# Moving a transform table's second half and its transposes to a later place in the opening of a fused FFT and channel-mix kernel

## The chip, the cores and the metric

The kernel runs on one core of a Trainium2 chip. The metric is device time in microseconds (us), the median of several executions. The kernel before takes 593.0 us.

## The reference

For x of 8 batches x 3072 positions x 256 channels: a real FFT along the positions, a complex matrix product with a soft threshold, the inverse FFT, then a channel mix in the manner of RWKV.

```python
X = np.fft.rfft(x, axis=1)
Yr = Xr @ w_r - Xi @ w_i + b_r            # and Yi = Xr @ w_i + Xi @ w_r + b_i
Yr = np.sign(Yr) * np.maximum(np.abs(Yr) - 0.01, 0.0)      # the same for Yi
x = np.fft.irfft(Y, n=3072, axis=1)
# channel mix: x_prev is x moved by one position
xk, xr = mu_k * x + (1 - mu_k) * x_prev, mu_r * x + (1 - mu_r) * x_prev
v = np.maximum(xk @ w_k, 0.0) ** 2 @ w_v
return v / (1.0 + np.exp(-(xr @ w_r)))
```

## The kernel before

The FFT of length 3072 is done as 96 x 32: a first stage with the 96-point table FT, a second with the table G (and G0 for the group of frequency zero), the product, an inverse second stage with the table GI (the transposes of G, scaled), and an inverse first stage. G is made in the kernel by two sines on ScalarE, one for each half; GI is made from it by 24 transposes on TensorE and three copies out of PSUM.

The program is written out by a small list scheduler in Python. Every piece of TensorE work is a `Unit` with what it needs, a due time and an assumed duration; the loop issues the unit with the earliest due time among those that are ready by the assumed clock. So assumed times do not change what is computed, but they set the order of instructions on every engine. Each unit takes one of four slots of PSUM and gives it back when its copy has run; `copy` gives that copy to ScalarE or VectorE, whichever is free first by the assumed clock. The parts that matter (cuts are marked `...`):

```python
    def make_g():
        nc.scalar.activation(G[:, :, :, 1, :], ang, AF.Sin, bias=0.0, scale=sc1)   # second sine
        nc.vector.tensor_scalar(out=G0[:, 0], in0=G[:, 0, 1], scalar1=-1.0, scalar2=None, op0=ALU.mult)
        nc.vector.tensor_copy(out=G0[:, 1], in_=G[:, 0, 0])
        nc.vector.memset(G0[:, 0:2, 0, 0:1], 0.0)
        nc.vector.tensor_copy(out=G0[:, 2:4], in_=G[:, 0])
    ...
    def table_gi(n):
        def issue(ps, h, end):
            for i in range(8):                                   # eight transposes of G
                nc.tensor.matmul(ps[:, 128 * i:128 * i + 128], G[:, 8 * n + i]..., ident, ...)
            def evac(k):
                nc.scalar.activation(GI[:, 8 * n:8 * n + 8, :], ps..., AF.Copy, bias=0.0, scale=float(1.0 / 32))
                ...
                if n == 0:                                       # two corrections of one row each
                    for r in (0, 64):
                        nc.vector.tensor_scalar(out=GI[r:r + 1, 0, :], in0=GI[r:r + 1, 0, :], scalar1=0.5, ...)
    def tables(k):
        nc.scalar.activation(G[:, :, :, 0, :], ang, AF.Sin, bias=0.0, scale=sc0)   # first sine
        at(run_on("act", k, 1.5) + 0.3, tables1)
    def tables1(k):
        make_g()
        e = run_on("act", k, 1.5)
        done["G"] = run_on("dve", e, 0.5)
    ...
    for q in range(4):
        done["x", 0, q] = 6.0 + 2.8 * q                          # assumed arrival of x, batch 0
    tab += [Unit(18.0 + n, 0.5, ["G"], table_gi(n)) for n in range(3)]
```

In batch 0 a piece of x goes through the first stage (L327 of the kernel before), its result is copied into the tile YT, 48 transposes in six units (L345) turn it, copies put them into the tiles A, then come the second stage (L370 and L387), a copy and a sign turn of XT (L397), the first product (L415), and z (L427) on VectorE. In the changed kernel the same lines have numbers lower by one.

## Time and profile before

| | kernel before |
|---|---|
| median, lowest, highest of 6 runs | 593.00, 592.49, 593.43 us |
| span of the profiled execution | 592.2 us |
| TensorE, VectorE, ScalarE busy | 566.3, 524.1, 420.2 us |
| TensorE without a matmul, 12.76 to 24 us | 1.53 us of 11.24 |
| VectorE starts on z of batch 0 | 25.40 us |

The span is the time from the first to the last instruction of one execution. "Busy" adds the instructions of one engine. The last two rows are about the opening, the only part that the change touches; the prediction below shows the lines that they come from. The profiled execution took 593.96 us by the clock outside, longer than each of the six timed runs.

### The profile page before, as it was taken

The numbers are of one execution on the slowest core, as the hardware profiler recorded it, in microseconds if no ns is written. First come the engines' busy times: TensorE is split into PE (matmuls) and PEld (weight loads), VectorE is DVE, ScalarE is ACT, GpSimd is POOL, SyncE is SP. The second block draws the span as 40 slices with busy tenths as digits, with TensorE's granted clock in tenths as the row PEclk, the third lists the DMA queues.
The fourth block names the chain that finished last, engine by engine and source line by source line (L and its number), as shares of the span: only waits on it lengthen the run. The fifth ranks groups of instructions, "written<-read, shape, count | busy, mean of one in ns | idle before, by whom it ended". The sixth has DMA issues, their size and how long they took to land.

```text
span 592.2 us, 12299 instructions
## 1 busy us (share of the span) xinstructions
PE 566.3 (96%) x4822; PEld 429.7 (73%) x4889; DVE 524.1 (89%) x833; ACT 420.2 (71%) x457; POOL 26.3 (4%) x56
## 2 busy tenths in 40 slices
PE   3999899999999999999999999999999999999996
PEld 3888666777767777677777777677877787776665
DVE  7799989798998889898998989988999889979883
ACT  4686967677777687676777677777776867767652
POOL 7101000000000000000000000000000000000000
PEclk9999999999999999999999999999999999999999
DMA  8976879724589365963478655683337722362223
GB/s 132 139 145 159 189 178 240 179 71 93 132 208 217 102 142 137 253 182 69 113 169 250 149 121 129 160 238 112 99 93 236 179 55 72 100 169 70 64 56 97
DMA packets 69594, 84.38 MB, mean 142 GB/s; under 512 B 9121, under 2 KB 54560, under 8 KB 69536
## 3 DMA queue, kind: packets, MB, share of 16 engines
q1 hardware_dynamic: 62912, 68.98, 41.7%
q0 software_dynamic: 6432, 14.36, 16.5%
q8 instruction: 38, 0.62, 0.4%
q10 hardware_dynamic: 192, 0.26, 0.2%
q14 instruction: 20, 0.16, 0.1%
HBM read 50.73 MB, written 47.19 MB: 165 GB/s over the span
## 4 chain that ended last, share of the span: by engine, by line
PE 82%; DVE 6%; ACT 5%; issue 2%; DMA 2%; SPq 1%; POOL 1%; POOLq 0%; DVEq 0%; ACTq 0%
PE banks L671 27%; PE banks L627 23%; PE banks L415 13%; PE banks L654 5%; PE banks L454 3%; PE banks L387 3%; PE banks L272 3%; ACT rl L633 2%; PE banks L535 2%; DMA Adr<-A 1%; ACT rg L659 1%; PE banks L345 1%; SPq L297 1%; DVE k L639 1%; DMA out_dram<-o 1%
## 5 line engine op out<-in xcount | busy, mean ns | idle before, releaser
L633 ACT ACTIVATE rl<-banks 128x1024 bf16<-128x1024 f32 x192 | 193.6, 1028 | 94.0 <-PE banks L627 88.2
L627 PE MATMUL banks<-xk,wk 128*128 128x512 bf16 x701 | 188.7, 379 | 5.3 <-DVE xk L600 0.7
L671 PE MATMUL banks<-wv,k 128*128 128x256 bf16 x1536 | 183.0, 272 | 0.4 <-ACT rl L633 0.3
L671 PEld LDWEIGHTS <-k 128*128 128x128 bf16 x1536 | 149.3, 98 | 29.0 <-issue 1.4
L639 DVE TENSOR_TENSOR k<-rl 128x1024 bf16<-128x1024 bf16 x192 | 130.5, 685 | 13.9 <-ACT rl L633 13.9
L627 PEld LDWEIGHTS <-wk 128*128 128x128 bf16 x768 | 73.9, 98 | 60.7 <-issue 3.1
L415 PEld LDWEIGHTS <-XT 128*128 128x128 bf16 x768 | 74.5, 98 | 15.5 <-DVE XT L397 0.3
L415 PE MATMUL banks<-wi,XT 128*128 128x256 bf16 x384 | 73.3, 273 | 0.0
L415 PE MATMUL banks<-wr,XT 128*128 128x256 bf16 x384 | 73.3, 272 | 0.0
L600 DVE SCALAR_TENSOR_TENSOR xk<-diff,muk,YT 128x512 bf16<-128x512 bf16 x96 | 69.1, 745 | 0.2
L600 DVE SCALAR_TENSOR_TENSOR xr<-diff,mur,YT 128x512 bf16<-128x512 bf16 x96 | 68.8, 745 | 0.0
L682 DVE TENSOR_TENSOR o<-banks,rg 128x1024 f32<-128x1024 f32 (+1 forms) x49 | 58.6, 1197 | 3.7 <-PE banks L671 3.4
L219 ACT ACTIVATE YT<-banks 128x768 bf16<-128x768 f32 x56 | 42.7, 829 | 10.8 <-PE banks L535 7.9
L219 ACT ACTIVATE XT<-banks 128x1024 bf16<-128x1024 f32 (+2 forms) x45 | 42.8, 956 | 10.6 <-PE banks L387 10.6
L654 PE MATMUL banks<-wrm,xr 128*128 128x256 bf16 x384 | 49.8, 272 | 0.1
L659 ACT ACTIVATE rg<-banks 128x1024 bf16<-128x1024 f32 x48 | 49.1, 1023 | 0.0
L432 ACT ACTIVATE z<-banks 128x1024 bf16<-128x1024 f32 x32 | 32.7, 1022 | 19.9 <-PE banks L415 19.8
L654 PEld LDWEIGHTS <-xr 128*128 128x128 bf16 x384 | 37.2, 98 | 11.6 <-issue 0.2
L219 ACT ACTIVATE V<-banks 128x1024 bf16<-128x1024 f32 x35 | 35.9, 1025 | 13.5 <-PE banks L454 12.8
L219 ACT ACTIVATE A<-banks 96x1024 bf16<-96x1024 f32 (+1 forms) x39 | 39.3, 1021 | 7.3 <-PE banks L272 6.0
L594 DVE TENSOR_TENSOR diff<-YT 128x1024 bf16<-128x1024 bf16 x48 | 32.8, 683 | 3.7 <-ACT YT L219 3.7
L444 DVE TENSOR_TENSOR Y<-z,Y 128x1024 bf16<-128x1024 bf16 x48 | 33.2, 693 | 1.7
(90 smaller groups left out, 443.1 us busy)
## 6 DMA issues: line engine op xcount, KB each, us to landing
out_dram<-o SPq DMA_DIRECT2D x188, 128.0 KB, 2.2
xs<-in_x_dram POOLq DMA_DIRECT2D x32, 384.0 KB, 6.2
Vdr<-V SPq DMA_DIRECT2D x192, 64.0 KB, 1.8
V<-Vdr SPq DMA_DIRECT2D x32, 384.0 KB, 6.5
Adr<-A SPq DMA_DIRECT2D x24, 384.0 KB, 5.4
A<-Adr SPq DMA_DIRECT2D x48, 192.0 KB, 4.4
wk<-in_moe_w_k_dram POOLq DMA_DIRECT2D x1, 512.0 KB, 15.1
wv<-in_moe_w_v_dram POOLq DMA_DIRECT2D x1, 512.0 KB, 15.9
```

Of the source, the lines that this page charges most:

```text
L219: nc.scalar.activation(out, in_, AF.Copy, bias=0.0, scale=1.0)
L415: nc.tensor.matmul(o, lhs, w[:, c, :], start=(w is wr and c == 0), stop=(w is wi and c == NCD - 1))
L444: nc.vector.tensor_tensor(out=y, in0=z, in1=y, op=ALU.subtract)
L594: nc.vector.tensor_tensor(out=df, in0=y, in1=yp, op=ALU.subtract)
L600: nc.vector.scalar_tensor_tensor(out=m[:, c, :], in0=df[:, c, :], scalar=mu[:, c:c + 1], in1=yp[:, c, :], op0=ALU.mult, op1=ALU.add)
L627: nc.tensor.matmul(ps[:, 512 * f:512 * f + 512], wk[:, c, 128 * ff:128 * ff + 128], xk[:, c, :], start=(c == 0), stop=(c == NCD - 1))
L633: nc.scalar.activation(rl, ps, AF.Relu, bias=0.0, scale=1.0)
L639: nc.vector.tensor_tensor(out=k2, in0=rl, in1=rl, op=ALU.mult)
L654: nc.tensor.matmul(ps[:, 256 * q:256 * q + 256], xr[:, c, 128 * q:128 * q + 128], wrm[:, c, :], start=(c == 0), stop=(c == NCD - 1))
L659: nc.scalar.activation(rg, ps, AF.Sigmoid, bias=0.0, scale=1.0)
L671: nc.tensor.matmul(ps[:, 256 * q:256 * q + 256], K2[t][:, ff, 128 * q:128 * q + 128], wv[:, ff, :], start=(ff == 0), stop=(ff == NCF - 1))
L682: nc.vector.tensor_tensor(out=o[:, lo:hi], in0=ps[:, lo:hi], in1=rg[:, lo:hi], op=ALU.mult)
```

## The change

The intent: to let the data's transposes start as soon as the data is there, instead of behind the table's. The second sine is issued as before, but the four G0 instructions of VectorE are put behind it in a step of their own; x of batch 0 is assumed to arrive every 2.55 instead of 2.8 us; and the table's transposes also wait, in the schedule, for the last copy of the first stage.

```diff
--- before.py
+++ after.py
@@ -155,8 +155,7 @@
     G = const.tile([128, NG, 2, 2, 32], FP16, name="G")
     G0 = const.tile([128, 4, 2, 32], FP16, name="G0")
 
-    def make_g():
-        nc.scalar.activation(G[:, :, :, 1, :], ang, AF.Sin, bias=0.0, scale=sc1)
+    def make_g0():
 
         nc.vector.tensor_scalar(out=G0[:, 0], in0=G[:, 0, 1], scalar1=-1.0, scalar2=None, op0=ALU.mult)
         nc.vector.tensor_copy(out=G0[:, 1], in_=G[:, 0, 0])
@@ -737,9 +736,12 @@
         at(run_on("act", k, 1.5) + 0.3, tables1)
 
     def tables1(k):
-        make_g()
-        e = run_on("act", k, 1.5)
-        done["G"] = run_on("dve", e, 0.5)
+        nc.scalar.activation(G[:, :, :, 1, :], ang, AF.Sin, bias=0.0, scale=sc1)
+        at(run_on("act", k, 1.5), tables2)
+
+    def tables2(k):
+        make_g0()
+        done["G"] = run_on("dve", k, 0.5)
 
     P = 71.5
     START = 50.0
@@ -777,7 +779,7 @@
                             [("k2", t, i) for i in range(4)] + [("rg", t)], v_unit(t, p), part=p))
 
     for q in range(4):
-        done["x", 0, q] = 6.0 + 2.8 * q
+        done["x", 0, q] = 6.0 + 2.55 * q
         load_x(1, q)
         done["x", 1, q] = 19.0 + 3.0 * q + (4.0 if q > 1 else 0.0)
         if q == 1:
@@ -787,7 +789,7 @@
     done["FT"], done["bias"] = 5.0, 21.0
     at(12.0, tables)
     tab = [Unit(18.0, 0.1, ["FT"], table_fi)]
-    tab += [Unit(18.0 + n, 0.5, ["G"], table_gi(n)) for n in range(3)]
+    tab += [Unit(18.0 + n, 0.5, ["G", ("x1", 0, 3, 1)], table_gi(n)) for n in range(3)]
     streams = [tok, val, fa, fb, fc, tab]
     at(START - 10.0, lambda k: mix_tokens(0, k))
```

## The prediction

> **What bounds the kernel now.** I read the page's head first, for which engine fills the span.
>
> ```profile
> span 592.2 us, 12299 instructions
> ...
> PE 566.3 (96%) x4822; PEld 429.7 (73%) x4889; DVE 524.1 (89%) x833; ACT 420.2 (71%) x457; POOL 26.3 (4%) x56
> ```
>
> TensorE is busy for 566.3 of 592.2 us, so all its idle time is 25.9 us. The change only touches how the tables G, G0 and GI are made, once, in the first 25 us. So next I cut the span into stretches (columns: stretch, its length, then busy time of PE, PEld, DVE, ACT, POOL, the granted clock, DMA share, GB/s).
>
> ```profile
> 12.76:24.00 11.24, 9.71 (x110) 9.20 (x110) 8.20 (x15) 9.56 (x10) 3.93 (x6) 1.00 1.11 95
> 24.00:45.00 21.00, 19.53 (x239) 17.09 (x237) 19.85 (x29) 15.34 (x18) 0.00 (x0) 1.00 0.83 163
> ...
> 145.00:520.00 375.00, 370.95 (x3078) 279.79 (x3124) 340.19 (x529) 276.22 (x299) 7.10 (x14) 1.00 0.58 149
> ```
>
> From 145 to 520 us TensorE is idle for only 4.05 us of 375. A microsecond won before 25 us therefore reaches the end, and nothing later can be won. The stretch that the change rewrites, 12.76 to 24 us, has 11.24 - 9.71 = 1.53 us of idle TensorE. Third, the chain that ended last, in that stretch (start, us, what):
>
> ```profile
> 12.66 0.98 ACT G L736
> 13.64 0.50 issue
> 14.14 1.57 ACT G L159
> 15.71 0.05 issue
> 15.76 1.89 PE banks L717 x16
> 17.64 3.34 PE banks L345 x32
> 20.98 0.22 PE banks L370 x2
> 21.20 0.93 PE banks L387 x14
> 22.12 0.60 PE banks L717 x8
> 22.72 0.89 PE banks L345 x16
> 23.62 1.76 PE banks L415 x16
> 25.38 0.02 issue
> 25.40 1.24 DVE z L427
> ```
>
> The reader is to see the order: both sines on ScalarE (L736, L159), then 16 of the 24 table transposes (L717), then the transposes of the data (L345), the second stage (L370, L387), and the first product (L415). TensorE stands still for 1.53 us until the second sine ends. The number to beat is 25.40, where VectorE starts on the first product's result; the next chain hangs on that.
>
> Fourth, the groups by form, first of 15.7 to 20.8 us, then of 20.8 to 27.5 us:
>
> ```profile
> L345 PE MATMUL banks<-ident,YT 128*128 128x128 f16 x32 | 3.5, 311 | 0.0
> L717 PE MATMUL banks<-ident,G 128*128 128x128 f16 x16 | 1.9, 312 | 1.5 <-ACT G L159 1.5
> ```
>
> ```profile
> L387 PE MATMUL banks<-G,A 128*128 128x128 f16 x22 | 1.7, 219 | 0.0
> ```
>
> The same 128x128 product takes 312 ns early and 219 ns later. Spacing matters more: 16 + 32 products fill 15.76 to 20.87 us, 5.11 / 48 = 0.107 us each, while the 8 that start at 22.12 have the next group's first start at 22.56 in the timeline: 0.44 / 8 = 0.055 us each. A unit of eight transposes so costs 0.85 us early and 0.44 us later.
>
> **What the Trainium skill says.** "TensorE: Matmul & The Clock Gate", part 1, the clock gate: matmuls of 128 columns come every 106.7 ns while the array is cold and every 55.6 ns once warm, and the array warms after some 3.4 us of sustained activity, in windows that run freely and do not start with the kernel. The trace agrees in the two spacings; the array warms at about 20.7 us, 4.9 us after the dense work began at 15.76, which fits one whole busy window plus a part of one. The granted clock in the table above reads 1.00 throughout and does not show it. The same page's table of specifications says that ScalarE and VectorE execute strictly in order. That is what lets a late table instruction hold up a data instruction; the trace shows each engine's instructions in the order of the program. "ScalarE: Activation LUTs", "Table sets: the hidden batching unit", says that cheap functions such as copy are in every set; so copies may stand between the two sines without a new table load. The trace agrees: sine, copy and sine alternate there with one load of 1.28 us at 0.74 us and the next at 42.74 us, for the sigmoid.
>
> **The change, part by part.** The order listing, with line numbers made equal, has the same instructions in the same number on every engine; GpSimd and the DMA queue have the same order, and TensorE, VectorE and ScalarE differ only up to the first product of batch 0. Nothing is removed or added.
>
> (1) ScalarE takes the copy of the third x piece before the first sine and the copy of the fourth between the sines. The first sine cannot move up: it waits for the angle that VectorE finishes at 12.63 us. The copy's matmuls end at about 11.75, so it runs 11.79 to 12.6 (0.8 us) and the sine starts at 12.66 as before. The second sine slips from 14.14 to 14.84 and ends at 16.4.
>
> (2) VectorE is relieved of one of three copies of 0.95 us. The fourth x piece ends on TensorE at 14.22; ScalarE copies one half 14.14 to 14.93, VectorE the other 14.26 to 15.21. Before, that last copy ran at 16.14 to 17.09, behind the G0 instructions.
>
> (3) So L345 starts at 15.27 in the place of L717 at 15.76: 0.49 us earlier. All 48 data transposes go first, six units of 0.85 us if cold: 15.27 to 20.39. Copies follow: VectorE's first 16.37 to 17.6, then the G0 group of 0.45 us, units 4 and 6 at 18.93 to 20.16 and 20.64 to 21.87; ScalarE's at 17.22 to 18.24, 18.14 to 19.16 and 19.78 to 20.80.
>
> (4) L370 runs at 20.39 to 20.61 (warm assumed), its copy on ScalarE 20.84 to 21.45; six L387 to 20.94, copy to 22.2. Then the first eight L717 wait for a PSUM slot, that of data unit 5, free at 20.80: 20.95 to 21.4. Sixteen of the 24 transposes are now warm: 16 x (0.107 - 0.055) = 0.83 us of TensorE time is saved, and 0.49 of an earlier start. That is 1.3 us, if TensorE stayed the bound.
>
> (5) It does not. Three GI copies on ScalarE, one every 0.92 us, come behind the XT copy at 22.2: the first ends at 23.14. The first product (L415) takes the slot which that copy frees, so it starts at 23.2, against 23.45 before. And VectorE now has in its order: two corrections of GI (0.44 us, waiting for that same copy), then the sign turn of XT (0.26), a copy of 1.23 and another turn of 0.28. From 23.18 these end at 23.6, 23.85, 25.05 and 25.25. L415 needs the turn only at its seventh matmul, at 23.86, so it is hardly delayed and ends at 25.1. VectorE is free for z at 25.25. Against 25.40 that is a gain of 0.15 us.
>
> From there the orders are the same, so I carry 0.15 us to the end, and add 0.1 for waits that I rounded up: 592.96 - 0.25 = 592.7 us.
>
> **The rivals.** *The full gain.* If ScalarE's table copies fit into its idle time, TensorE would stay the bound and 1.3 us would come through: 591.7. For it: ScalarE is idle 1.7 us of the 11.2 in this stretch, and TensorE's total work is less. Against it: the GI copies stand ahead of what the first product waits for, in both engines' order; in the kernel before two of the three were done by 18.8 us, while TensorE was busy with data. I give it one in six.
>
> *The wait turns into a loss.* If the array warms later, at 22 us instead of 20.7, L370, L387 and the first L717 run cold, about 0.5 us more on the chain of (4) and (5): 593.2. For it: the free-running window, and TensorE now has short gaps at 20.4 to 23.2, where before it was dense. Against: 15.27 to 20.39 alone holds a full window in most phases. One in four. The three runs of the kernel before, 592.49 to 593.43, spread by 0.94 us, as much as a window's phase could explain.
>
> *A transfer hides it.* The first wait for x in the chain is untouched, as the DMA order is. The loads of the next batch arrive before TensorE asks at 35.7 us, so a lead of some tenths should not hit them. If it did, the result would be 592.96 again.
>
> **Range and chances.** 0.15 to 0.25 us is under the spread of one kernel's runs. I take plus 0.8 and minus 0.9 around 592.7: 591.8 at the low end (nearly the full gain), 593.5 at the high end (late warming and a slow median). A change of 2% would be 11.9 us; all idle TensorE time before 45 us is under 12, and 6.3 of that is before any data. So faster by over 2%: 0.003; slower by over 2%: 0.003, only if the order broke something far later; within 2%: 0.994.
>
> **What would show it.** Step 1: second sine starts near 14.85. Step 3: first L345 near 15.3, with no L717 before it. Step 4: all 24 L717 at 219 ns rather than 314. Step 5: the GI corrections on VectorE waiting for ScalarE, and the first L415 at about 23.2, z at about 25.25. The busy sum of TensorE should fall by some 16 x 0.1 = 1.6 us at most, since the products overlap, without the span following. The prediction is wrong if z starts before 24.7 or after 25.8, if an instruction order differs after 26 us, or if a gain or loss at 28 us is not the same at 145 us.

## The result, and the profile after

| | before | after |
|---|---|---|
| median of 6 runs | 593.00 us | 592.71 us |
| lowest to highest | 592.49 to 593.43 | 592.30 to 593.16 |
| span of the profiled execution | 592.2 us | 591.0 us |
| data transposes in full pace of issue from | 17.43 us, behind 16 of the table's | 15.35 us, nothing ahead |
| first product starts | 23.45 us | 22.74 us |
| z starts | 25.40 us | 25.01 us |

The ratio is 0.9995, with a 95% interval of 0.9983 to 1.0008: the same time. All ratios here are the mean time of one kernel's fast runs over that of the other's of the same rounds, so not quite the ratio of the medians that I quote.

The same stretch of the chain that ended last, in the changed kernel (start, us, what):

```profile
14.34 0.97 DVE YT L220
15.31 0.05 issue
15.35 4.18 PE banks L344 x39
19.54 0.02 issue
19.56 0.69 ACT A L218
20.25 0.23 issue
20.48 1.29 ACT XT L218 x2
21.77 0.93 ACT GI L720
22.70 0.02 issue
22.72 0.43 DVE GI L726
23.15 0.01 issue
23.17 0.19 DVE GI L726
23.36 0.01 issue
23.37 0.27 DVE XT L396
23.64 0.05 issue
23.69 1.28 PE banks L414 x10
24.97 0.04 issue
25.01 1.23 DVE z L426
```

Before, this chain ran on TensorE from 15.76 to 25.38 without a break. Now TensorE leaves it at 19.5, and it goes through ScalarE's copies (A, XT, the first GI), VectorE's two corrections of GI and the sign turn of XT, and comes back for the last ten matmuls of the product. The start moved by 15.76 - 15.35 = 0.41 us and z by 0.39: what came off TensorE's path was handed to the two other engines, and about the earlier start was kept. That the two numbers agree so well is partly chance: the array reached full pace at 19.25 us here and at 20.82 in the profile before, which helped, and a correction of GI was held up by some 0.25 us, which hurt. Both are taken up below.

Pairing the instructions on VectorE by order shows what became of it. z and what follows come 0.39 to 0.42 us earlier up to 77 us. Then, between 77 and 85 us, the distance grows to 1.22, and it stays at 1.19 to 1.23 to the end (but for one entry at 425 us). The second step is not the change. It is a wait of the kernel before; first ScalarE's timeline of that kernel, then of a second execution of the same kernel (the run b_again below):

```profile
69.35 1.02 ACT L432 ACTIVATE z<-banks 128x1024 bf16<-128x1024 f32 x1
71.09 1.02 ACT L219 ACTIVATE V<-banks 128x1024 bf16<-128x1024 f32 x1 [0.72 <-DMA Vdr<-V]
```

```profile
69.34 1.02 ACT L432 ACTIVATE z<-banks 128x1024 bf16<-128x1024 f32 x1
70.26 1.02 ACT L219 ACTIVATE V<-banks 128x1024 bf16<-128x1024 f32 x1
```

In the first, a copy into the tile V waits 0.72 us for an earlier V to be stored; in the second it does not, and the span is 591.3 instead of 592.2 us. So the 1.2 us between the first two profiles would have been a false reading: 0.4 of it belongs to the change.

### The profile page after: what moved, and what is told of

Its sections match the earlier page's. It is cut to its first block, busy times and chain, and to the rows that moved or that the text cites. A ratio compares the mean times of both kernels' runs of the same rounds, so it can differ in the third digit from the quotient of the medians.

```text
span 591.0 us, 12301 instructions
## 1 busy us (share of the span) xinstructions
PE 566.1 (96%) x4822; PEld 429.1 (73%) x4889; DVE 522.4 (88%) x831; ACT 421.0 (71%) x459; POOL 26.7 (5%) x56
## 4 chain that ended last, share of the span: by engine, by line
PE 84%; ACT 6%; DVE 4%; issue 2%; DMA 2%; POOL 0%; SPq 0%; DVEq 0%; POOLq 0%; ACTq 0%
PE banks L670 28%; PE banks L626 24%; PE banks L414 14%; PE banks L653 5%; PE banks L453 4%; PE banks L271 3%; PE banks L386 3%; ACT rl L632 3%; PE banks L534 2%; ACT rg L658 2%; DMA xs<-in_x_dram 1%; PE banks L344 1%; DVE YT L220 1%; DMA out_dram<-o 1%; DVE z L426 1%
## 5 line engine op out<-in xcount | busy, mean ns | idle before, releaser
L653 PE MATMUL banks<-wrm,xr 128*128 128x256 bf16 x384 | 49.8, 272 | 0.1
L220 DVE CAST A<-banks 96x1024 bf16<-96x1024 f32 (+1 forms) x21 | 25.5, 1221 | 11.4 <-PE banks L271 9.4
```

Source lines behind the costliest of these rows:

```text
L653: nc.tensor.matmul(ps[:, 256 * q:256 * q + 256], xr[:, c, 128 * q:128 * q + 128], wrm[:, c, :], start=(c == 0), stop=(c == NCD - 1))
```

## The experiments

Twelve kernels ran, each five times or, where the table says so, six; all gave correct results and all their runs counted as fast. The widest were after_warm_late_w, with two of its six at 594.78 and 595.32 us, and after_defer, with one at 597.07. They went out in four jobs, whose kernels shared a chip and the runs of the kernel before: b_again, a_again, only_later and only_split; after_fix_pool, after_defer, before_warm and after_warm; only_spacing, after_late_w and after_warm_late_w; after_warm_v5.

| run | median us | kernel before, same rounds | ratio, 95% interval | first product | z |
|---|---|---|---|---|---|
| b_again | 592.89 | 592.98 | 0.9999, 0.9987 to 1.0012 | 23.44 | 25.39 |
| a_again | 592.13 | 592.98 | 0.9988, 0.9975 to 1.0002 | 22.69 | 24.70 |
| only_later | 594.93 | 592.98 | 1.0037, 1.0025 to 1.0050 | 23.30 | 25.31 |
| only_split | 594.54 | 592.98 | 1.0026, 1.0013 to 1.0038 | 23.12 | 25.07 |
| only_spacing (6 runs) | 593.65 | 593.20 | 1.0006, 0.9993 to 1.0019 | 23.81 | 25.75 |
| after_fix_pool | 592.18 | 592.98 | 0.9985, 0.9973 to 0.9998 | 22.50 | 24.50 |
| after_defer | 594.09 | 592.98 | 1.0028, 1.0009 to 1.0046 | 21.04 | 24.22 |
| before_warm | 592.10 | 592.98 | 0.9983, 0.9969 to 0.9996 | 22.20 | 24.15 |
| after_warm | 591.97 | 592.98 | 0.9981, 0.9969 to 0.9994 | 21.27 | 23.45 |
| after_late_w | 592.20 | 593.20 | 0.9981, 0.9968 to 0.9994 | 22.42 | 24.43 |
| after_warm_late_w (6 runs) | 592.11 | 593.20 | 0.9992, 0.9970 to 1.0015 | 21.27 | 23.28 |
| after_warm_v5 | 592.82 | 593.00 | 0.9989, 0.9975 to 1.0003 | 21.30 | 23.57 |

The last two columns are single profiles. In after_late_w, after_warm_late_w and only_spacing the kernel before had two runs at 594.3 and 594.6 among eleven, which makes those ratios a little too low.

### Both kernels again

b_again and a_again are the two kernels with no edit.

> The kernel before, unchanged, for a second look and more times. The pair of profiles so far puts the first z of batch 0 at 25.40 us before and 25.01 after, and a further 0.82 us apart between 71 and 85 us. Theory 1 (the order of the instructions sets the gain): z again at 25.3 to 25.5, the ratio to itself 1.000 within 0.001. Rival 1 (the phase of the array's warming set it): the array warms at another time than 20.7 us (the transposes go from 314 to 219 ns), and z moves with half of the shift, anywhere from 24.7 to 26. Rival 2 (the 0.82 us is a transfer that happens to be late in one execution): ScalarE's copy of V does not wait 0.7 us for a store at 71 us this time, and the time of the span is near 591.4 in place of 592.2.

> The changed kernel, unchanged, once more. Theory 1: z at 24.9 to 25.3 again whatever the array does, since copies and not TensorE bind after 20 us; ratio of times 0.9993 (0.4 us of 593). Rival 1: z moves between 24.6 and 25.6 with the warming, which was at 19.2 us in the first profile, and the ratio over five rounds is 1.000. Rival 2: if the wait at 71 us belongs to the order before the change, it is absent here again and the ratio is 0.998 (1.2 us); if it is chance, it appears in some executions of both and the ratio stays at 0.9993.

The kernel before puts z at 25.39 again, and the wait at 71 us is gone: rival 2 holds, that wait is chance. The changed kernel puts z at 24.70 this time, below what theory 1 gave it, although its array reached full pace later (near 20 us, against some 19.2 in its first profile). So the later warming went with the earlier z, against the sign of rival 1. That does not refute it yet, since two more things differ; after_late_w below sets profiles side by side in which little but the warming does. Against b_again, a_again is 0.69 us ahead at z and 0.68 to 0.70 us ahead nearly everywhere to the end, with no second step. In this pair a lead of the opening is carried through.

These are the two things that differ between the two profiles of the changed kernel. The last piece of x reached TensorE at 12.38 instead of 12.77 us, and its copy on VectorE ended earlier; so the transposes went on from 14.97 and not from 15.35. The kernel before can't use that: its TensorE waits for the second sine, which ends at 15.71 whenever x comes. But little of this earlier start got through: with the later warming, ScalarE's first copy of GI began at 21.61 us against 21.65. And the two corrections of GI took 0.38 us in place of 0.63, which makes up most of the 0.30 us at z. First the profile of the changed kernel, GpSimd and then VectorE:

```profile
21.50 0.73 POOL L170 DMA_DIRECT2D wrm<-in_moe_w_r_dram  x1 [3.79 <-DMA bias<-in_b_i_dram]
22.22 0.92 POOL L170 DMA_DIRECT2D wv<-in_moe_w_v_dram  x1
```

```profile
22.72 0.63 DVE L726 TENSOR_SCALAR GI<-GI 1x128 f16<-1x128 f16 x2 [1.42 <-ACT GI L720]
23.37 0.26 DVE L396 TENSOR_SCALAR XT<-XT 128x384 bf16<-128x384 bf16 x1
```

Then the same in a_again:

```profile
21.84 0.91 POOL L170 DMA_DIRECT2D wv<-in_moe_w_v_dram  x1 [0.33 <-DMA bias<-in_b_i_dram]
```

```profile
22.67 0.38 DVE L726 TENSOR_SCALAR GI<-GI 1x128 f16<-1x128 f16 x2 [1.17 <-ACT GI L720]
23.07 0.26 DVE L396 TENSOR_SCALAR XT<-XT 128x384 bf16<-128x384 bf16 x1
```

The reader is to compare ends: where the first correction took 0.43 us (the chain above shows it alone), GpSimd was issuing the load of wv from 22.22 to 23.14, and the correction ended at 23.15. In a_again that issue was nearly over at 22.75. The Trainium skill, "SBUF — State Buffer", "Who interferes with whom", says that VectorE and GpSimd share one pair of ports, that an instruction of VectorE in a mode that uses both its ports contends with GpSimd, and that whichever issues first keeps the pair for its whole instruction. That the correction is in such a mode was not shown; the numbers fit it, and after_late_w tests whether the issue is the cause.

### The parts one at a time

only_later is the kernel before with the third part of the change alone:

```diff
-    tab += [Unit(18.0 + n, 0.5, ["G"], table_gi(n)) for n in range(3)]
+    tab += [Unit(18.0 + n, 0.5, ["G", ("x1", 0, 3, 1)], table_gi(n)) for n in range(3)]
```

> Only the transposes of the table are held back until the data's first stage is done; both sines still run back to back and the G0 group still stands ahead of the last copy of the first stage on VectorE. Theory 1: the data transposes then start only after that copy, at 17.3 us as before, with nothing on TensorE from 14.2 to 17.3; z at 26.3 to 26.8, about 1 to 1.3 us later than before, ratio 1.002. Rival (the later transposes are what gains, the VectorE order is a detail): z at 25.0 as in the whole change, ratio 0.9993.

only_split is the changed kernel with the old assumed arrival and the old need:

```diff
-        done["x", 0, q] = 6.0 + 2.55 * q
+        done["x", 0, q] = 6.0 + 2.8 * q
-    tab += [Unit(18.0 + n, 0.5, ["G", ("x1", 0, 3, 1)], table_gi(n)) for n in range(3)]
+    tab += [Unit(18.0 + n, 0.5, ["G"], table_gi(n)) for n in range(3)]
```

> The G0 group is issued later on VectorE, behind the last copy of the first stage, but the assumed arrival of x is left as before, so both sines still run back to back on ScalarE and VectorE still makes three of the first stage's copies. The transposes of the table fall behind the data's by themselves. Theory 1: the last ScalarE copy of the first stage ends at 16.4 as before, so the data transposes start at 16.45 us, 1.1 us later than with the whole change: z at 25.9 to 26.3, ratio 1.001. Rival (the copy between the sines does not matter): z at 25.0, ratio 0.9993.

only_spacing is the kernel before with the assumed arrival alone:

```diff
-        done["x", 0, q] = 6.0 + 2.8 * q
+        done["x", 0, q] = 6.0 + 2.55 * q
```

> Only the assumed arrival of x is changed, as in the whole change; the four G0 instructions are still issued together with the second sine, and nothing holds back the table's transposes. ScalarE then takes the third copy before the first sine and one copy between the sines, but VectorE meets the G0 group, which waits for the second sine's end at 16.4, with no copy of the first stage behind it. Theory (the copies' places and the G0 group's place have to change together): eight table transposes come first, at 15.0 to 16.5, TensorE's order is between the two kernels, z at 25.0 to 25.6, ratio 0.9990 to 1.0005. Rival (the copies alone bring the gain): z at 24.7, ratio 0.9987 as in the whole change. Second rival, from the two halves tried before: a worse order later in batch 0, ratio 1.002 to 1.004.

None of the three gains any time. The longer times of only_later and only_split are clear of noise, only_spacing's is not. My expectations for z were wrong in all three, and the reasons teach something.

In only_later the data transposes do start in earnest at 17.14, as expected, but z comes at 25.31 and not after 26.3. The schedule put only 32 of the 48 data transposes ahead of the first product; the other 16 were pushed in later, eight inside the second product and eight behind the third. The same happened in only_split: its TensorE timeline has them in the middle of batch 0.

```profile
26.19 0.61 PE L344 MATMUL banks<-ident,YT 128*128 128x128 f16 x8
...
30.16 0.61 PE L344 MATMUL banks<-ident,YT 128*128 128x128 f16 x8
```

That makes z early and the rest late. Against b_again, only_split is 0.32 us ahead at z, and 2.96 us behind at the fifth z; 1.6 of it remains to the end (1.87 in only_later). From 28 to 52 us its TensorE is busy for 21.46 us against 22.53 in b_again. A single mark in the opening is therefore no measure of a variant whose order changes behind the mark. For the changed kernel itself it is one, since its order differs from the kernel before only up to the first product.

In only_spacing ScalarE does take a copy between the sines, but by the assumed clock it also takes the very last copy of the first stage, behind the second sine, 16.27 to 17.07 us; eight of the table's transposes run meanwhile, the data transposes start in full pace of issue at 17.25, and z comes at 25.75. So the earlier copies need the G0 group moved out of VectorE's way, which then takes the last copy instead.

A listing of the instructions shows one more thing without a run: the changed kernel with the third part left out gives the same order on all five engines as with it. The third part of the change has no effect beside the other two.

### What binds behind the transposes

after_fix_pool gives the two corrections to GpSimd:

```diff
-                        nc.vector.tensor_scalar(out=GI[r:r + 1, 0, :], in0=GI[r:r + 1, 0, :], scalar1=0.5,
+                        nc.gpsimd.tensor_scalar(out=GI[r:r + 1, 0, :], in0=GI[r:r + 1, 0, :], scalar1=0.5,
```

> The changed kernel, with the two one-row corrections of GI on GpSimd instead of VectorE. In the changed kernel VectorE stood still for 1.2 to 1.4 us at 21.3 to 22.7 us until the first GI copy came, and the sign turn and the copy of XT stood behind it. Theory (the in-order corrections hold the chain up): the turn runs at 21.8 to 22.1 instead of 23.1 to 23.4, the first product is no longer held up at its seventh matmul, and z starts 0.3 us earlier for the same arrival of x: 24.4 to 24.7. Rival (the PSUM slot that the first GI copy frees is what binds): the first product still starts at 22.7, z at 24.5 at best, and since x's arrival alone moves it by 0.3 us, no difference in time can be seen: ratio to the kernel before 0.9985 to 0.9995 either way.

The sign turn runs at 21.57 instead of 23.07 or 23.37, the first product goes through without its pause, and z comes at 24.50. In the two profiles of the changed kernel, weight loads of TensorE had waited 0.41 and 0.16 us for that turn. The corrections were part of the chain, but no more than that: the product starts at 22.50, when the first GI copy frees its slot, and z follows two microseconds later, as fast as 16 matmuls allow. z is inside its expected range, but a_again is no clean partner for it, since the array was warm at 18.95 us here and at 19.95 there. Beside after_late_w below, which was warm at 18.69 and leaves the corrections on VectorE undisturbed, z is no earlier: 24.50 against 24.43. The time (0.9985) can't be told from a_again's (0.9988).

after_defer moves the table's transposes and GI copies behind the products:

```diff
+                if b == 0 and half == 0:
+                    done["mix", u] = end
...
-                needs = [("y", b, u), "GI"]
+                needs = [("y", b, u), ("GI", u // 2)]
...
-                if n == 2:
-                    done["GI"] = e
+                done["GI", n] = e + (0.5 if n == 0 else 0.0)
...
-    tab += [Unit(18.0 + n, 0.5, ["G", ("x1", 0, 3, 1)], table_gi(n)) for n in range(3)]
+    tab += [Unit(18.0 + n, 0.5, ["G", ("mix", 2 * n)], table_gi(n)) for n in range(3)]
```

> The changed kernel, with the transposes and copies of the GI table moved behind the first products of batch 0: eight each after the products 0, 2 and 4, each inverse asking for its third of the table alone. Theory (the three GI copies on ScalarE and the slots they hold are what binds between 20 and 23 us): the first product starts at 21.4 to 21.8 in place of 22.7 and z at 23.3 to 23.7; the 24 transposes cost TensorE 1.3 us later, so about 0.3 to 0.8 us are left at the end, ratio 0.9975 to 0.9985 to the kernel before. Rival (the copies only fill idle time of ScalarE; what binds is the data's own copies): the first product moves by less than 0.3 us and the end gets later by 0.5 to 1 us, ratio 1.0005.

The first product starts at 21.04, 1.65 us before a_again's: the GI copies and their slots did bind it. But z comes at 24.22 and not at 23.5, because of the next thing in VectorE's order: a copy of XT from PSUM, 21.38 to 22.60, now stands ahead of the sign turn, and the product waits for that at 22.91. And the later order pays the lead back twice over: 0.8 us ahead at the third z, 2.5 behind at the fifth, ratio 1.0028. So the theory was right about the mechanism and wrong about its worth. What of the later loss comes from the table's transposes and what from the displaced units was not taken apart.

### The cold array

before_warm and after_warm put 36 matmuls of the identity with itself into TensorE's waits for x, into slots that the next real matmuls overwrite. The edit of after_warm (before_warm has the last 14 ahead of the table's transposes):

```diff
+                for i in range((0, 12, 5, 5)[q] if b == 0 and c == 0 else 0):
+                    nc.tensor.matmul(ps[:, 0:128], ident, ident, start=True, stop=True)
                 for i in range(8):
                     nc.tensor.matmul(pv[:, i, :], xt[:, i, 128 * c:128 * c + 128], FT, start=True, stop=True)
...
+                for i in range(14 if b == 0 and u == 0 else 0):
+                    nc.tensor.matmul(ps[:, 0:128], ident, ident, start=True, stop=True)
                 for i in range(4):
                     for c in range(NCD):        # the data transposes
```

> The kernel before, with 36 matmuls of the identity by itself put into TensorE's waits between the pieces of x and ahead of the table's transposes, into the slots that the next real matmuls overwrite; results unchanged. Theory (TensorE at half pace bounds the kernel before from 15.76 to 20.7 us): the array is warm by 15 us, the 16 transposes of the table take 0.9 instead of 1.7 us, and the first z comes at 24.2 to 24.6 instead of 25.4: ratio 0.998. Rival (copies bind there as well): z earlier by less than 0.4 us. If the activity in the waits is not enough, the array warms no earlier than 19 us and the time is the same or up to 0.3 us longer.

> The changed kernel with the same 36 matmuls, the last 14 ahead of the first data transposes. Theory of the prediction (once 48 cold transposes are past, copies on ScalarE and VectorE bind): a warm array shortens the 48 from 5.1 to at least 2.7 us, but the six copies behind them take 0.9 to 1.2 us each on two engines, so z moves from 24.7 to 25.0 to 23.5 to 24.0 and not by the whole 2.4 us; ratio 0.997 to 0.998. Rival (the copies bind from the first transposes on): z at 24.5 or later, ratio 0.999.

In the four profiles with these fillers the array becomes warm between 9.6 and 12.1 us. Groups of TensorE by form, 15.7 to 20.8 us of before_warm, to set beside the 311 and 312 ns in the prediction:

```profile
L347 PE MATMUL banks<-ident,YT 128*128 128x128 f16 x32 | 2.1, 219 | 0.3 <-DVE YT L221 0.3
L389 PE MATMUL banks<-G,A 128*128 128x128 f16 x14 | 1.1, 218 | 0.4 <-DVE A L221 0.4
L721 PE MATMUL banks<-ident,G 128*128 128x128 f16 x16 | 1.1, 220 | 1.3 <-ACT G L159 1.3
```

z moves to 24.15 in the first kernel and to 23.45 in the second, both 0.05 us below the expected ranges: 1.24 and about 1.25 to 1.56 us earlier. Two conclusions follow. The kernel before was bound in good part by TensorE at half pace, as the prediction read it, but not all the way: 48 matmuls at 0.055 instead of 0.107 us would give 2.5 us, and b_again, warm at 20.17 us against 20.82 in the first profile, has z at the same place, with a copy of A on VectorE (20.23 to 21.47) in its chain. And the six units of data transposes, which take 3.06 us here and took 5.20 in a_again, give back only 1.25 of those 2.14 us at z, since ScalarE's and VectorE's copies bind. In the chain of after_warm TensorE's transposes don't appear at all:

```profile
14.91 1.46 ACT G L743
16.38 0.59 ACT A L218
16.97 0.22 issue
17.18 1.51 ACT A L218 x2
18.70 0.30 issue
18.99 1.31 ACT XT L218 x2
20.30 0.92 ACT GI L724
21.23 0.04 issue
21.27 1.96 PE banks L418 x16
```

With a warm array in both, the change is worth 24.15 - 23.45 = 0.70 us at z, against 0.69 between a_again and b_again and 0.39 in the first pair. These are single profiles, and z in them also moves with the arrival of x and with GpSimd's issues; so the 0.70 shows that the change still pays with a warm array, not that its worth is the same whenever the array warms.

### Loads issued by GpSimd

after_late_w takes the changed kernel and has GpSimd issue the loads of wrm and wv only after the second inverse of batch 0:

```diff
-    big["wrm"] = load_w("wrm", moe_w_r, NCD, D)
-    big["wv"] = load_w("wv", moe_w_v, NCF, D)
...
+                    if b == 0 and u == 1:
+                        nc.gpsimd.tensor_copy(out=n1c[0:128], in_=vt[:, 0, 0:1])
+                        big["wrm"] = load_w("wrm", moe_w_r, NCD, D)
+                        big["wv"] = load_w("wv", moe_w_v, NCF, D)
```

> The changed kernel, with the two last weight loads (wrm, wv) issued by GpSimd only after the second inverse of batch 0, near 31 us, instead of at 20.8 to 23.1 us. They are first used near 70 and 77 us. Theory (GpSimd's issuing of a load holds up VectorE's table corrections when the two meet: 0.43 us for the first in the profile where the issue ran at 22.22 to 23.14, 0.19 in the one where it ended at 22.75): the two corrections take 0.38 us together, z starts at 24.7 for an unwarmed array at 20 us, and no product of batch 0 has to wait for them beyond that; ratio 0.9985 to 0.9990. Rival (the difference of 0.3 us between the two profiles of the changed kernel came from the array's warming or x's arrival): z at 24.7 to 25.0 with the corrections at 0.38 or 0.63 us as before, unrelated to GpSimd. If the loads come too late, the gates' product near 69 us waits and the time rises by 1 us or more.

With no issue beside them the corrections take 0.38 us, the product starts at 22.42 and z at 24.43.

```profile
22.40 0.38 DVE L731 TENSOR_SCALAR GI<-GI 1x128 f16<-1x128 f16 x2 [1.32 <-ACT GI L725]
```

Set against the first profile of the changed kernel, whose array warmed at nearly the same time, z is 0.58 us earlier. The corrections start 0.32 us sooner, from the earlier data, and take 0.25 us less. The loads still came in time: no gate or value product waits for them. Some 0.63 us appeared in two profiles: the first of the changed kernel, where an issue covered the first correction, and after_warm_v5 below, where one covered both. It was 0.38 us in b_again, a_again, only_later, only_split and this one, where the two hardly met or not at all. after_warm_v5, GpSimd and then VectorE:

```profile
21.20 0.73 POOL L170 DMA_DIRECT2D wrm<-in_moe_w_r_dram  x1 [3.48 <-DMA bias<-in_b_i_dram]
```

```profile
21.28 0.64 DVE L730 TENSOR_SCALAR GI<-GI 1x128 f16<-1x128 f16 x2 [1.66 <-ACT GI L724]
```

Its first correction ran at its usual 0.18 us inside the issue, and only the second, from 21.47, took 0.44 and ended with the issue at 21.92. So not every overlap delays: this one, and a sign turn of after_fix_pool (21.57 to 21.83 us, in an issue from 21.51 to 22.23), started within 0.1 us of an issue's begin and went through. In after_warm the second sign turn took 0.45 us, starting at 23.07 beside an issue that ran to 23.41, and 0.29 us in after_warm_late_w without it. The other instructions there are alike, so I count the collision as shown.

The same profile settles rival 1 of the two repeats. after_late_w and a_again start their transposes at the same 14.97 us, and their corrections take the same 0.38 us, but the array was warm at 18.69 us here and at 19.95 in a_again. (The last copy of the first stage even ended 0.23 us later here.) ScalarE's copies of GI, a_again first:

```profile
21.61 2.87 ACT L720 ACTIVATE GI<-banks 128x1024 f16<-128x1024 f32 x3
```

```profile
21.32 2.88 ACT L725 ACTIVATE GI<-banks 128x1024 f16<-128x1024 f32 x3
```

They come 0.29 us earlier, the first product and z 0.27 us (22.42 and 24.43 against 22.69 and 24.70). So the phase of the warming does move z in the changed kernel, by 0.27 us for 1.26, less than the half that rival 1 gave it.

### The candidate, and where the lead goes

after_warm_late_w joins the two edits just shown, and after_warm_v5 is after_warm with two more buffers for the tile V and the same order on every engine:

```diff
-    r1_pool, ym_pool, v_pool, v2_pool = pool("r1p", 2), pool("ymp", 3), pool("vp", 3), pool("v2p", 4)
+    r1_pool, ym_pool, v_pool, v2_pool = pool("r1p", 2), pool("ymp", 3), pool("vp", 5), pool("v2p", 4)
```

> The changed kernel with the 36 filling matmuls and the late weight loads together, the candidate for the best version. Theory: array warm by 13 us, z at 23.2 to 23.4 (0.1 to 0.2 before that of the filling matmuls alone, whose second sign turn took 0.45 instead of 0.29 us beside a load being issued), ratio 0.996 to 0.9975. Rival (the lead is lost again later to transfers, since the five times of the filling matmuls alone spread over 1.6 us and their median was only 1.0 us below the kernel before although the first z came 1.9 us earlier): z as said, yet the ratio stays at 0.998, and a profile shows a wait for a store or a load in batches 0 to 2 that the kernel before does not have.

> The changed kernel with the 36 filling matmuls (weight loads in their old place), and five instead of three buffers for the tile V, whose copies on ScalarE and VectorE wait for the stores of an earlier V. The order of every engine is the same as with the filling matmuls alone. Theory (some executions lose the lead because a copy into V waits for a store to land: 0.7 us at 71 us in one profile of the kernel before, 1.3 us at 39 us in the profile of the candidate with late loads, whose array then fell back to half pace from 42 to 46 us): no copy into V waits for a store, the five times lie within 0.8 us, and the median is 1.4 to 1.9 us below the kernel before, ratio 0.9968 to 0.9977. Rival (the spread comes from somewhere else, the waits for stores are rare): the ratio is 0.998 again, with a spread above 1 us.

z comes at 23.28 and 23.57 (the 0.28 us between them is, but for 0.02, the correction that GpSimd's issue held up in after_warm_v5), and still the times are no better than after_warm's: 0.9992 and 0.9989. The profile of after_warm_late_w fell on an execution of 594.78 us. It is 2.1 us ahead of b_again at 30.7 us and 0.07 behind at 49.8. ScalarE's timeline there:

```profile
39.58 1.02 ACT L218 ACTIVATE V<-banks 128x1024 bf16<-128x1024 f32 x1 [1.30 <-DMA Vdr<-V]
```

and the stretches of the same execution (columns as in the prediction's table; the granted clock is the third from the end):

```profile
40.00:43.00 3.00, 1.98 (x26) 1.54 (x26) 2.03 (x3) 2.98 (x4) 0.00 (x0) 0.89 0.41 112
43.00:46.00 3.00, 3.00 (x31) 2.98 (x29) 1.86 (x3) 2.31 (x4) 0.00 (x0) 0.55 0.32 86
46.00:50.00 4.00, 3.99 (x54) 3.52 (x52) 3.97 (x6) 2.52 (x4) 0.00 (x0) 1.00 0.56 154
```

A copy into V waited 1.30 us for a store, TensorE stood idle for 1.8 us behind it, and its granted clock then fell to 0.55 for 43 to 46 us. Two more such waits (0.90 us at 71 us, 1.1 us later on) and a load of V that came late at 252 us followed, and by the end it was 1.74 us behind. With five buffers no copy into V waits for a store in the profile, so that expectation held. But the lead of 1.83 us was kept only to 190 us and shrank to 0.28 by 273 us. TensorE's waits from 180 to 275 us in after_warm_v5:

```profile
PE banks L373 <- DMA A<-Adr: 0.7, 1, 0.7
PE banks L538 <- DMA V<-Vdr: 0.7, 1, 0.7
PE banks L373 <- DMA out_dram<-o: 0.4, 1, 0.4
```

So the rival holds: the spread comes from more places than the store of V. In some executions a transfer lands late, of whatever kind, and takes from the lead. Four profiles (a_again, after_fix_pool, after_late_w, after_warm) carried their lead over b_again to the end within 0.1 us. before_warm lost 0.24 us of its 1.24, behind a load of V that came late at 250 us, and the two here lost more. What makes a transfer late in one execution and not in another stays open.

No version is clearly the best. after_warm has the lowest median (591.97 us), before_warm, after_warm_late_w, a_again, after_fix_pool and after_late_w follow within 0.23, and their intervals overlap.

## Why the prediction was right or wrong

**The verdict and the size** were right: 592.71 us measured, 592.7 predicted, and over a second set of rounds 592.13, also inside the range. The 11 runs of the changed kernel in the two sets have a mean of 592.53. That the first median met 592.7 to 0.01 us is luck: neither interval (0.9983 to 1.0008 and 0.9975 to 1.0002) excludes that nothing changed. The gain shows in the traces alone, and in the first pair they gave 0.39 us at z in place of 0.15.

**Steps 1 and 2, the copies and the sines:** right. The second sine started at 14.81 (14.84 predicted), VectorE's last copy at 14.34 (14.26). The listing that the prediction quotes is misread in one point: the number of instructions is not the same on every engine, as two copies go from VectorE (833 to 831) to ScalarE (457 to 459). The step itself has one of them.

**Step 3, the start of the transposes:** right, 15.35 against 15.27. What the step did not say is that this start follows the arrival of x; in a_again it was 14.97.

**Step 4, what TensorE saves:** wrong in its accounting. It took 16 table transposes out of the slow phase and counted 0.83 us as saved. But as many data transposes took their places: the slow phase ends at some moment, not after some number of table matmuls, and before and after it was filled with matmuls of the same size. TensorE's busy sum fell from 566.30 to 566.11 us, by 0.2 and not by up to 1.6, and between b_again and a_again it rose from 565.76 to 566.06, although all 24 table transposes ran at the fast 219 ns in both profiles, as predicted. So the rival of the full gain, 1.3 us, was built on a saving that did not exist; there was only the earlier start, 0.41 us in that pair of profiles. The prediction came out right because step 5 did not rest on it.

**Step 5, the copies and corrections bind:** right in mechanism, shown by the chain after, by after_fix_pool and by after_defer. The sizes were off in both directions: the first product started at 22.74 (23.2 predicted, in part because the array was warm by 19.4 and not at 20.4), the corrections took 0.63 us (0.44 predicted, GpSimd's issue), and z came at 25.01 (25.25). So 0.39 us came through in place of 0.15, with two errors against each other: the earlier warming, which was the luck of that execution, and the held-up correction.

**The rival of a loss through late warming** did not occur, because the array happened to warm earlier than in the profile before, and not later. The cost itself is real: 0.27 us for 1.26 us of delay between after_late_w and a_again, where the rival had put about 0.5 us on 1.3. **The rival of a transfer that hides it** is half right. The loads of the next batch did not hide it, but stores and loads further on can, in some executions.

**Carrying the lead to the end:** right in the pair a_again and b_again, -0.69 us at z and -0.68 to -0.70 nearly throughout. The first pair failed the prediction's own sign (0.39 us at 28 us, 1.22 at 145), because its kernel before met a late store. And that TensorE is nearly always busy later on does not by itself carry a lead: after_warm_v5 lost 1.5 us of its lead on the way.

## What to carry to other kernels

When work is moved off a bound engine, ask what steps into its place there, and which in-order queue receives the rest: here a table's copies and two corrections of one row each became the new chain, and little more than the earlier start was gained. A part of a change to a schedule, taken alone, can be worse than either kernel, and one mark in the opening does not tell. And before reading a gain of a tenth of a per cent from two profiles, pair the instructions and see where the distance jumps: here a jump far from the change was one execution's late transfer.

## What the Trainium skill lacked or had wrong

- "SBUF — State Buffer", "SBUF: two separate sides", warns that VectorE can hold up GpSimd's issue of a load. The reverse follows from the lock as the page states it, but the issue of a load as the one that holds up VectorE is not spelled out, and was what cost time here: a correction of 128 elements on VectorE took 0.43 instead of 0.19 us beside a load being issued (0.92 us of GpSimd), ending 0.01 us after it.
- The same page, "Who interferes with whom", says that the second to issue is fully blocked for the other's whole instruction. Beside two small corrections on GpSimd (1.19 us together, from 23.17 us, in after_fix_pool) a sign turn of VectorE that started at 23.23 took 0.38 instead of 0.29 us. That is less than a full block. Nor did a load's issue block for its whole length: in after_warm_v5 a correction ran from 21.28 to 21.46 us inside an issue of 21.20 to 21.93 without delay. Times on GpSimd are rough in the profile, so I leave it as a doubt.
- "TensorE: Matmul & The Clock Gate", part 1, gives some 3.4 us of sustained activity for warming, but not how much idle time a window may hold. Here the pieces of x alone (16 matmuls of 96x96 in about 1.5 us out of every 1.9 from some 9 us on) did not warm the array by 14 us; with 36 fillers of 128x128 it became warm between 9.6 and 12.1 us. Whether the idle time or the smaller matmuls kept it cold was not taken apart. In the ten unfilled profiles it warmed only after the transposes began, at 18.7 us at the earliest.
- The same part warns that throttle events in a trace can't be fully trusted. It does not say in which way; here the granted clock of the profile reads 1.00 in the opening, while the spacing of matmuls is 0.107 us and not 0.055; it did show the later fall, 0.55 at 43 to 46 us of after_warm_late_w.
